# One statically planned instruction stream for two mixed attention branches, in place of two phases with a filler list

## The chip, the cores and the metric

The kernel runs on one core of a Trainium2 chip. The metric is the device time of one execution in microseconds (us), from the first instruction to the last. A core has five engines that run side by side, each through its own instruction stream in order: TensorE (PE in the profile, its weight loads PEld), ScalarE (ACT), VectorE (DVE), GpSimd (POOL) and the queue that issues transfers (SP).[...]

## The reference

The input is one sequence of 2048 tokens with 640 features; there are 32 heads of 20. Branch A is a linear attention whose feature map is a softmax over each head's 20 features, of `+p` and of `-p`. Branch B is causal attention within four segments of 512 tokens, mixed with a memory that is updated from segment to segment. A gate per token mixes the two.

```python
# A: q,k,v = x @ wqkv ; pq = q @ w_phi ; pk = k @ w_phi      (per head)
phi_q = concat([softmax(pq), softmax(-pq)], -1)
phi_k = concat([softmax(pk), softmax(-pk)], -1)
kv  = einsum('bhsf,bhsd->bhfd', phi_k, v);  z = phi_k.sum(s)
o   = (phi_q @ kv) / (phi_q @ z + 1e-6);    a = o.reshape(B,S,D) @ wo
# B: for each of 4 segments of L=512
logits = q k^T * Dh**-0.5 + mask            # mask: -1e9 above the diagonal
a_dot  = softmax(logits) @ v
a_mem  = phi(q) @ M / (phi(q) @ z + 1e-6)   # phi(t) = t+1 if t>0 else exp(t)
o = g_h * a_mem + (1 - g_h) * a_dot
M += phi(k)^T v ;  z += phi(k).sum           # then b = o @ wo
out = gate * a + (1 - gate) * b              # gate = sigmoid((x * gate_w).sum(-1))
```

## The kernel before

It works in two phases. Phase one loads and transposes x, folds `w_phi` into the k and q weights of A, and runs A over the 16 chunks of 128 tokens (`a1_v`, `a1_k`, `a1_kv`). Phase two is a loop over 32 steps, one for each segment and each group of four heads of B; the order of TensorE's stream is written by hand, and units of other work (the projections of the next segment, A's second half, the output projection) are put between its parts from a list sorted by a position. The order on the other engines is left to the framework.

```python
def mm_x(ps, sc, W, lo, hi):                      # one projection of 128 tokens, 5 matmuls
    for c in range(KC):
        nc.tensor.matmul(ps, lhsT=xT[:, c, sc * P:(sc + 1) * P], rhs=W[:, c, lo:hi],
                         start=(c == 0), stop=(c == KC - 1))
...
def b_k(s, c):                                    # K of B: project, store, load transposed
    for hf in range(2):
        ps = wtile("kb_ps")
        mm_x(ps[:, 0:320], sc, WkB, 320 * hf, 320 * hf + 320)
        nc.vector.tensor_copy(out=kp[:, hf * 16:hf * 16 + 16, 0:DH], in_=...)
    nc.sync.dma_start(out=kd[s][rows, :], in_=kp.rearrange("p h d -> p (h d)"))
    nc.sync.dma_start_transpose(out=kT2[s % 2][:, :, rows], in_=kd[s][rows, :])
...
def b_q(s, g):                                    # Q of B comes out transposed from TensorE
    ps = wtile("qb_ps")
    for c in range(KC):
        nc.tensor.matmul(ps, lhsT=WqB[:, c, 4 * g:4 * g + 4, :],    # heads padded 20 -> 32
                         rhs=xT[:, c, s * L:(s + 1) * L], ...)
    nc.vector.tensor_copy(out=qT, in_=ps)
...
POFF = {0: 0, 1: 512, 3: 896, 2: 1024}
def b_qk(qT, kT, PT, cs):                         # called with (0,), (1, 3), (2,)
    st2 = [pst.tile([P, 2, 512], F32, name="st") for _ in range(2)]   # pst: 2 x 2 banks
    for c in cs:
        for i in range(4):                        # four heads, 32 rows of the array each
            nc.tensor.matmul(st2[i // 2][:, i % 2, o:o + n], lhsT=kT[r:r + 32, ...],
                             rhs=qT[r:r + 32, c * P:L], ..., tile_position=(r, 0))
    for pr in range(2):
        nc.scalar.activation(out=PT[:, 2 * pr:2 * pr + 2, base:base + w],
                             in_=st2[pr][:, :, 0:w], func=ACT.Exp, scale=SCALE_B)
    for c in cs:                                  # causal mask of the diagonal block
        view = PT[:, :, POFF[c]:POFF[c] + P]
        nc.gpsimd.affine_select(out=view, in_=view, pattern=[[0, 4], [1, P]],
                                compare_op=ALU.is_ge, fill=0.0, base=0,
                                channel_multiplier=-1)
def b_pv(...):   # 40 matmuls of 21 columns: lhsT a 128x128 block of PT, rhs = [v, 1]
def b_mem(...):  # 4 matmuls read the memory M, 4 update it, and two small VectorE operations
...
def a3_pq(s, g):   # 6 groups of 6 heads: 5 matmuls of 512 columns, then exp(+), exp(-)
def a3_num(...):   # numerator and denominator of A in one set of matmuls, 22 columns a head
def fin_mm(...):   # 10 matmuls of 320 columns, a ScalarE copy, the store of the output
...
for k in range(NG):                               # 32 steps
    for t, cs in enumerate(((0,), (1, 3), (2,))):
        b_qk(qT, kT, PT, cs)
        if t == 0 and k + 1 < NG:
            nxt = b_q(*divmod(k + 1, G))
        ...                                       # b_mem / b_pv / b_epi of step k-1
        while fill and fill[0][0] < k + SHARE[t]:
            fill.pop(0)[1]()
```

Of the kernel before, what the change touches and what calls it, by code (L numbers as in the profile page):

```python
# [11 lines left out]
AX = mybir.AxisListType  # L12

@with_exitstack
def kernel(
# [16 lines left out]
    P = 128  # L32
    S = 2048
    D = 640
    H = 32
    DH = 20
    KC = D // P
    NCH = S // P
    NSEG = 4
    L = S // NSEG  # L40
    G = H // 4
    SCALE_B = DH ** (-0.5)
    NG6 = 6
    GW = [120] * 5 + [40]
    GH = [6] * 5 + [2]
    EKW = 1376
    V1 = DH + 1

    x2 = A_x[0]
    out2 = out[0]  # L50
    PSUM = bass.MemoryType.PSUM

    class Seg:
        pass

    const = ctx.enter_context(tc.tile_pool(name="const", bufs=1))
    bres = ctx.enter_context(tc.tile_pool(name="bres", bufs=1))
    bkw = ctx.enter_context(tc.tile_pool(name="bkw", bufs=2))
    dram = ctx.enter_context(tc.tile_pool(name="dram", bufs=1, space=bass.MemoryType.DRAM))
    kd = [dram.tile([L, H * 32], BF16, name=f"kd{s}") for s in range(NSEG)]  # L60
    od = [[dram.tile([L, D], BF16, name=f"od{s}_{X}") for X in range(2)] for s in range(NSEG)]
    psw = ctx.enter_context(tc.tile_pool(name="psw", bufs=4, space=PSUM))
    psa_stack = ExitStack()
    psa = psa_stack.enter_context(tc.tile_pool(name="psa", bufs=1, space=PSUM))
    apool_stack = ExitStack()
    apool = apool_stack.enter_context(tc.tile_pool(name="apool", bufs=1, side="right"))
    a1w = apool_stack.enter_context(tc.tile_pool(name="a1w", bufs=3, side="right"))
    ctx.enter_context(tc.manual_schedule(engines={mybir.EngineType.PE}))

    def wtile(name, dt=F32):  # L70
        if dt == BF16:
            return psw.tile([P, 1024], BF16, name=name, tag="w")
        return psw.tile([P, 512], F32, name=name, tag="w")

    xT = const.tile([P, KC, S], BF16, name="xT")
    xv = x2.rearrange("(c p) d -> p c d", p=P)
    x_nat = apool.tile([P, 4, D], BF16, name="x_nat")
    wnat_k = apool.tile([P, KC, D], BF16, name="wnat_k")
    wnat_q = apool.tile([P, KC, D], BF16, name="wnat_q")
    Wc = apool.tile([P, NG6, DH], BF16, name="Wc")  # L80
    WvA = apool.tile([P, KC, D + 1], BF16, name="WvA")
    gw_row = apool.tile([KC, P], BF16, name="gw_row")
    beta_b = const.tile([P, H], BF16, name="beta_b")
    WkB = bres.tile([P, KC, D], BF16, name="WkB")
    WvB = bres.tile([P, KC, D], BF16, name="WvB")
    WqB = bres.tile([P, KC, H, 32], BF16, name="WqB")
    WoA = bres.tile([P, KC, D], BF16, name="WoA")
    WoB = bres.tile([P, KC, D], BF16, name="WoB")
    wphi_rows = A_w_phi.rearrange("h f g -> (h f) g")
    nc.vector.memset(Wc[:, NG6 - 1, :], 0.0)  # L90

    def wload(dst, src):
        nc.sync.dma_start(out=dst, in_=src.rearrange("(c p) n -> p c n", p=P))

    nc.sync.dma_start(out=x_nat[:, 0:2], in_=xv[:, 0:2, :])
    nc.sync.dma_start(out=gw_row, in_=gate_w.rearrange("(c p) -> c p", p=P))
    nc.sync.dma_start(out=Wc[0:120, 0:5, :],
                      in_=wphi_rows[0:600, :].rearrange("(c p) g -> p c g", p=120))
    nc.sync.dma_start(out=Wc[0:40, 5, :], in_=wphi_rows[600:640, :])
    nc.sync.dma_start(out=x_nat[:, 2:4], in_=xv[:, 2:4, :])  # L100
    wload(WvA[:, :, 0:D], A_wqkv[:, 2 * D:3 * D])
    wload(wnat_k, A_wqkv[:, D:2 * D])
    for sc in range(4, NCH):
        nc.sync.dma_start_transpose(out=xT[:, :, sc * P:(sc + 1) * P],  # L104
                                    in_=x2[sc * P:(sc + 1) * P, :])
    wload(wnat_q, A_wqkv[:, 0:D])
    wload(WkB, B_wk)
    wload(WvB, B_wv)
    wq_st = []
    for c in range(KC):  # L110
        w = a1w.tile([P, D], BF16, name="wq_st", bufs=2)
        nc.sync.dma_start(out=w, in_=B_wq[c * P:(c + 1) * P, :])
        wq_st.append(w)
    wload(WoA, A_wo)
    wload(WoB, B_wo)
    nc.sync.dma_start(out=beta_b, in_=B_beta.partition_broadcast(P))

    ident_f = const.tile([P, P], F32, name="ident_f")
    nc.gpsimd.memset(ident_f, 0.0)
    nc.gpsimd.affine_select(out=ident_f, in_=ident_f, pattern=[[-1, P]],  # L120
                            compare_op=ALU.not_equal, fill=1.0, base=0,
                            channel_multiplier=1)
    ident_b = const.tile([P, P], BF16, name="ident_b")
    nc.vector.tensor_copy(out=ident_b, in_=ident_f)

    def block_mask(name, n, step, width, parts):
        m = const.tile([P, n], F32, name=name)
        nc.gpsimd.memset(m, 1.0)
        nc.gpsimd.affine_select(out=m, in_=m, pattern=[[-step, n]], compare_op=ALU.is_ge,
                                fill=0.0, base=0, channel_multiplier=1)  # L130
        nc.gpsimd.affine_select(out=m, in_=m, pattern=[[step, n]], compare_op=ALU.is_ge,
                                fill=0.0, base=width - 1, channel_multiplier=-1)
        return m

    m6 = block_mask("m6", 6, DH, DH, 120)
    bd4 = block_mask("bd4", 4, 32, 32, P)
    ind = const.tile([P, 4], BF16, name="ind")
    nc.vector.tensor_copy(out=ind, in_=bd4)

    EkNs = []  # L140
    for i in range(4):
        e = apool.tile([P, EKW], BF16, name=f"EkN{i}")
        nc.gpsimd.memset(e[:, 1280:EKW], 0.0)
        EkNs.append(e)
    WkA = apool.tile([P, KC, D], BF16, name="WkA")
    WqA = const.tile([P, KC, 728], BF16, name="WqA")
    nc.gpsimd.memset(WqA[:, :, D:728], 0.0)
    nc.gpsimd.memset(WqB[:, :, :, DH:32], 0.0)

    kpads = []  # L150
    for b in range(3):
        kp = bres.tile([P, H, 32], BF16, name=f"kpad{b}")
        nc.gpsimd.memset(kp[:, :, DH:32], 0.0)
        kpads.append(kp)
    kT2 = [bres.tile([P, G, L], BF16, name=f"kT{b}") for b in range(2)]
    phik2, vB2 = [], []
    for b in range(2):
        pk = bres.tile([P, 4, H, 32], BF16, name=f"phik{b}")
        vb = bres.tile([P, 4, H, V1], BF16, name=f"vB{b}")
        nc.gpsimd.memset(pk[:, :, :, DH:32], 0.0)  # L160
        nc.gpsimd.memset(vb[:, :, :, DH:V1], 1.0)
        phik2.append(pk)
        vB2.append(vb)
    Msb = bres.tile([P, G, 4, V1], F32, name="Msb")
    nc.gpsimd.memset(Msb, 0.0)
    nc.gpsimd.affine_select(out=Msb[:, :, :, DH], in_=Msb[:, :, :, DH],
                            pattern=[[0, G], [-32, 4]], compare_op=ALU.not_equal,
                            fill=1e-6, base=-DH, channel_multiplier=1)
    Mbd = bres.tile([P, G, 4, V1], BF16, name="Mbd")

    Wphi = apool.tile([P, NG6, 6, DH], BF16, name="Wphi")
    nc.vector.tensor_tensor(out=Wphi[0:120],
                            in0=Wc[0:120, :, None, :].to_broadcast([120, NG6, 6, DH]),
                            in1=m6[0:120, None, :, None].to_broadcast([120, NG6, 6, DH]),
                            op=ALU.mult)

    class Fold:
        pass

    def fold_new(wn, dst, nm):  # L180
        f = Fold()
        f.wn, f.dst = wn, dst
        f.WT = apool.tile([P, NG6, KC, P], BF16, name=f"WT{nm}", tag="WT")
        return f

    def fold_tr(f, g):
        gw = GW[g]
        tp = wtile("wtp", BF16)
        for ic in range(KC):
            nc.tensor.transpose(out=tp[0:gw, ic * P:(ic + 1) * P],  # L190
                                in_=f.wn[:, ic, g * 120:g * 120 + gw], identity=ident_b)
        src = tp[0:gw, 0:D].rearrange("p (c k) -> p c k", k=P)
        if g % 2 == 0:
            nc.scalar.copy(out=f.WT[0:gw, g], in_=src)
        else:
            nc.vector.tensor_copy(out=f.WT[0:gw, g], in_=src)

    def fold_mm(f, ic):
        for (g0, g1) in ((0, 4), (4, 6)):
            ps = wtile("wfold")  # L200
            for g in range(g0, g1):
                gw = GW[g]
                o = (g - g0) * 120
                nc.tensor.matmul(ps[:, o:o + gw], lhsT=f.WT[0:gw, g, ic, :],
# [519 lines left out]
```

The softmax here doesn't subtract the row's maximum and nothing guards it: scores larger than these inputs give would overflow.

## Time and profile before

| | |
|---|---|
| device time | 417.99 us, median of 3 runs (416.78 to 420.93) |
| span of the profiled execution | 415.1 us, 9891 instructions, mean granted TensorE clock 0.951 |
| instructions | 3930 matmuls, 503 on ScalarE, 608 on VectorE, 366 on GpSimd |
| transfers | 30.04 MB in 59137 packets; the one transfer queue fills 27.4% of the 16 engines' time |
| from memory / to memory | 7.24 MB read, 11.40 MB written |

How to read it: the profile gives each engine's busy time as a share of the span, the busy share in 40 equal slices (a digit is tenths), the chain of work that ended last, and groups of instructions with the time their engine stood idle just before them and what released it. A busy TensorE isn't a TensorE at its peak, since matmuls overlap and their ends are modelled.

### The profile page before, as it was taken

The page shows a single profiled execution, that of the slowest core. Times are in us where ns is not written, and L with a number is a line of the kernel's source. Part 1 is how long each engine was busy: PE and PEld are TensorE (multiplying, and loading weights), DVE is VectorE, ACT ScalarE, POOL GpSimd, SP SyncE. Part 2 cuts the span into 40 slices and gives each one's busy share as a digit, 9 for nine tenths or more (in the row PEclk, how much of TensorE's full clock was granted, in tenths as well). Part 3 has the DMA queues.
Part 4 walks back from the last instruction along what each step waited for, and adds up shares of the span by engine and source line. Part 5 has one row for each costly group of instructions (what it writes and reads, how often), then busy time and mean ns, then how long its engine had stood idle before and what let it go on. Part 6 is the DMA issues. An engine that isn't in the chain of part 4 may idle for free.

```text
span 415.1 us, 9891 instructions
## 1 busy us (share of the span) xinstructions
PE 340.2 (82%) x3930; PEld 215.7 (52%) x3961; DVE 234.2 (56%) x608; ACT 271.7 (65%) x503; POOL 209.1 (50%) x366
## 2 busy tenths in 40 slices
PE   2996999967788858789889888789988798876686
PEld 1674777755344534445455545356554355444454
DVE  4336856769246635557587456376664555466620
ACT  1573666721777757888677886568877597976402
POOL 9026797891225444545545454353554464657510
PEclk9998999999999989899999999899998899999659
DMA  8887000005301204217211213821020162100311
GB/s 235 145 251 260 2 3 2 2 25 153 77 26 27 54 14 86 49 59 151 72 51 48 53 49 105 148 73 53 30 56 2 34 159 65 49 13 5 112 42 55
DMA packets 59137, 30.04 MB, mean 72 GB/s; under 512 B 45779, under 2 KB 57043, under 8 KB 59091
## 3 DMA queue, kind: packets, MB, share of 16 engines
q1 hardware_dynamic: 59091, 29.41, 27.4%
q8 instruction: 31, 0.51, 0.5%
q14 instruction: 15, 0.12, 0.1%
HBM read 7.24 MB, written 11.40 MB: 45 GB/s over the span
## 4 chain that ended last, share of the span: by engine, by line
PE 42%; ACT 19%; DVE 13%; POOL 10%; SPq 6%; issue 5%; DMA 4%; POOLq 0%; DVEq 0%; ACTq 0%
ACT PT L431 14%; PE o_ps L578 10%; PE qb_ps L399 6%; SPq L104 4%; POOL PT L435 4%; PE st L425 4%; PE vb_ps L237 4%; PE pq_ps L503 4%; DMA wq_st<-in_B_wq_dram 3%; PE kb_ps L237 3%; PE nd_ps L445 3%; PE va_ps L237 2%; PE ka_ps L237 2%; POOL EkN L265 2%; DVE ts L541 2%
## 5 line engine op out<-in xcount | busy, mean ns | idle before, releaser
L431 ACT ACTIVATE PT<-st 128x1024 bf16<-128x1024 f32 (+1 forms) x192 | 158.4, 884 | 22.8 <-PE st L425 19.1
L435 POOL TENSOR_SCALAR_AFFINE_SELECT PT<-PT 128x512 bf16<-128x512 bf16 x128 | 80.6, 642 | 108.4 <-ACT PT L431 95.4
L237 PEld LDWEIGHTS <-xT 128*128 128x128 bf16 x640 | 61.2, 100 | 32.4 <-issue 3.3
L425 PE MATMUL st<-qT,kT 32*128 32x128 bf16 (+3 forms) x512 | 48.2, 313 | 21.0 <-ACT PT L431 18.9
L265 POOL TENSOR_TENSOR EkN<-Ek,krec 128x1280 bf16<-128x1280 bf16 x16 | 37.7, 2359 | 25.6 <-DVE krec L264 23.8
L445 PE MATMUL nd_ps<-vB,PT 128*128 128x21 bf16 x1280 | 42.8, 173 | 3.0 <-POOL PT L435 1.4
L403 DVE CAST qT<-qb_ps 128x512 bf16<-128x512 f32 x32 | 22.1, 691 | 40.7 <-PE qb_ps L399 40.7
L578 PEld LDWEIGHTS <-oT 128*128 128x128 bf16 x320 | 32.2, 104 | 22.8 <-issue 4.1
L445 PEld LDWEIGHTS <-PT 128*128 128x128 bf16 x1280 | 36.7, 96 | 14.0 <-issue 6.1
L399 PE MATMUL qb_ps<-xT,WqB 128*128 128x512 bf16 x146 | 40.1, 396 | 4.5 <-DVE ts L541 2.6
L425 PEld LDWEIGHTS <-kT 32*128 32x128 bf16 x512 | 15.6, 92 | 50.3 <-issue 47.6
L546 POOL TENSOR_TENSOR oA<-ts 128x360 bf16<-128x360 f32 (+1 forms) x32 | 27.5, 861 | 25.9 <-DVE ts L541 24.8
L582 ACT CAST osb<-o_ps 128x320 bf16<-128x320 f32 x32 | 13.6, 425 | 38.3 <-PE o_ps L578 37.9
L578 PE MATMUL o_ps<-WoA,oT 128*128 128x320 bf16 x160 | 29.7, 320 | 4.6 <-ACT Eq L507 1.6
L503 PE MATMUL pq_ps<-xT,WqA 128*128 128x512 bf16 x103 | 29.6, 388 | 3.9 <-DVE tm L482 1.6
L578 PE MATMUL o_ps<-WoB,oT 128*128 128x320 bf16 x160 | 30.2, 324 | 2.9 <-DMA oT<-od 2.9
L237 PE MATMUL vb_ps<-WvB,xT 128*128 128x320 bf16 x160 | 25.8, 310 | 5.4 <-DVE Msb L469 2.1
L541 DVE TENSOR_TENSOR ts<-num_ps,cs 128x360 f32<-128x360 f32 (+1 forms) x64 | 28.4, 483 | 2.1
L478 DVE RECIPROCAL rd<-nd_ps 128x16 f32<-128x16 f32 x32 | 8.0, 249 | 34.6 <-PE nd_ps L445 34.5
L247 ACT CAST vA<-va_ps 128x320 bf16<-128x320 f32 x32 | 13.6, 425 | 20.5 <-PE va_ps L237 20.5
L257 ACT ACTIVATE Ek<-ka_ps 128x320 bf16<-128x320 f32 x64 | 23.1, 440 | 5.9 <-PE ka_ps L237 5.5
L237 PE MATMUL va_ps<-WvA,xT 128*128 128x320 bf16 (+1 forms) x160 | 26.8, 318 | 0.1
(109 smaller groups left out, 573.8 us busy)
## 6 DMA issues: line engine op xcount, KB each, us to landing
kd<-kpad SPq DMA_DIRECT2D x16, 256.0 KB, 2.4
od<-oA SPq DMA_DIRECT2D x16, 160.0 KB, 1.8
out_dram<-osb SPq DMA_DIRECT2D x16, 160.0 KB, 1.8
od<-oB SPq DMA_DIRECT2D x12, 160.0 KB, 2.2
WvA<-in_A_wqkv_dram SPq DMA_DIRECT2D x1, 800.0 KB, 5.6
wnat_k<-in_A_wqkv_dram SPq DMA_DIRECT2D x1, 800.0 KB, 7.4
wnat_q<-in_A_wqkv_dram SPq DMA_DIRECT2D x1, 800.0 KB
WkB<-in_B_wk_dram SPq DMA_DIRECT2D x1, 800.0 KB, 6.7
```

Source lines behind the costliest of these rows:

```text
L237: nc.tensor.matmul(ps, lhsT=xT[:, c, sc * P:(sc + 1) * P], rhs=W[:, c, lo:hi], start=(c == 0), stop=(c == KC - 1))
L257: nc.scalar.activation(out=Ek[:, sgn, 320 * hf:320 * hf + 320], in_=ps[:, 0:320], func=ACT.Exp, scale=1.0 if sgn == 0 else -1.0)
L265: nc.gpsimd.tensor_tensor(out=EkNs[sc % 4][:, 0:1280].rearrange("p (h f) -> p h f", f=DH), in0=Ek.rearrange("p s (h f) -> p (s h) f", f=DH ...
L399: nc.tensor.matmul(ps, lhsT=WqB[:, c, 4 * g:4 * g + 4, :], rhs=xT[:, c, s * L:(s + 1) * L], start=(c == 0), stop=(c == KC - 1))
L425: nc.tensor.matmul(st2[i // 2][:, i % 2, o:o + n], lhsT=kT[r:r + 32, c * P:(c + 1) * P], rhs=qT[r:r + 32, c * P:L], start=True, stop=True, ...
L431: nc.scalar.activation(out=PT[:, 2 * pr:2 * pr + 2, base:base + w], in_=st2[pr][:, :, 0:w], func=ACT.Exp, scale=SCALE_B)
L435: nc.gpsimd.affine_select(out=view, in_=view, pattern=[[0, 4], [1, P]], compare_op=ALU.is_ge, fill=0.0, base=0, channel_multiplier=-1)
L445: nc.tensor.matmul(nd[:, j * 84 + i * V1:j * 84 + (i + 1) * V1], lhsT=PT[:, i, o:o + P], rhs=vb[:, c, 4 * g + i, :], start=(j == 0 and i = ...
L503: nc.tensor.matmul(ps, lhsT=WqA[:, c, g * 120:g * 120 + P], rhs=xT[:, c, s * L:(s + 1) * L], start=(c == 0), stop=(c == KC - 1))
L541: nc.vector.tensor_tensor(out=ts[:, sgn, 0:nh, :], in0=pss[sgn][:, :, 0:DH], in1=cs[:, sgn, 0:nh, None].to_broadcast([P, nh, DH]), op=ALU. ...
L546: nc.gpsimd.tensor_tensor(out=segs[s].oA[qc][:, h0 * DH:(h0 + nh) * DH].rearrange("p (h d) -> p h d", d=DH), in0=ts[:, 0, 0:nh, :], in1=ts ...
L578: nc.tensor.matmul(ps[:, 0:320], lhsT=segs[s].oT[qc, X][:, k5, :], rhs=Wo[:, k5, hf * 320:hf * 320 + 320], start=(n == 0), stop=(n == 2 * ...
```

## The change

The change rewrites the kernel. Every piece of work becomes an operation with an engine (or a choice of ScalarE and VectorE), an assumed duration, a priority key and the tiles that it reads and writes. When the program is built, a list scheduler plays these durations forward and writes down one order for all engines; nothing of it runs on the chip. The purpose is to overlap branch B's attention, which needs ScalarE, with branch A's first half, which the kernel before had as a phase of its own.

```diff
+class Planner:
+    HOP = {"PE": 0.27, "ACT": 0.20, "DVE": 0.18, "POOL": 0.13, ...}   # assumed handover
...
+def pe_t(n):  return max(n / 2400 + 0.0025, 0.025)
+def act_t(n, psum=True): return (0.05 if psum else 0.093) + 0.000833 * n
...
-    psw = ctx.enter_context(tc.tile_pool(name="psw", bufs=4, space=PSUM))
-    pst = ctx.enter_context(tc.tile_pool(name="pst", bufs=2, space=PSUM, ...))   # later
-    ctx.enter_context(tc.manual_schedule(engines={mybir.EngineType.PE}))
+    st4 = ps.tile([P, 4, 512], F32, name="st4")
+    wt = [ps.tile([P, 512], F32, name=f"w{i}") for i in range(4)]
+    ctx.enter_context(tc.manual_schedule())
...
+    def b_kq(s, c, key):                     # K and Q of B, both by rows of tokens
+        for X, Wn in enumerate(("WkB", "WqB")):
+            for hf in range(2):
+                bk = proj(4 * s + c, Wn, (Wn,), hf, key)        # 5 matmuls of 320
+                op(AD, cp_t(320), copy_to(... T["kq"][i][..., X, :, 0:DH] ...))
+        dma(... kd[s][rows, :] <- T["kq"][i] ..., kb=524)
+    def kq_get(s, g, key):                   # 32 of these; [512, 256] -> [128, 2, 512]
+        dma(lambda: nc.sync.dma_start_transpose(out=T["kqT"][j],
+                                        in_=kd[s][:, g * 256:(g + 1) * 256]), ...)
...
+    def grp(s, g, i):                        # five score tiles for two groups of heads
+        return (((g, 0, 0),), ((g, 1, 0), (g, 3, 384)), ((g, 2, 0), (g + 1, 2, 256)),
+                ((g + 1, 0, 0),), ((g + 1, 1, 0), (g + 1, 3, 384)))[i]
+    def b_qk(n, s, prods, slot):             # 80 of these
+        ... nc.tensor.matmul(st4[:, i, o:o + w], ..., tile_position=(r, 0))
+        op("ACT", act_t(2048), lambda: nc.scalar.activation(
+            out=T["PT"][slot], in_=st4, func=ACT.Exp, scale=SCALE_B), ...)
+        for _, _, o in prods:
+                v = T["PT"][slot][:, :, o:o + P]
+                nc.gpsimd.affine_select(out=v[:, :, 0:8], in_=v[:, :, 0:8],
+                                        pattern=[[0, 4], [1, 8]],
+                                        compare_op=ALU.is_ge, fill=0.0, base=0,
+                                        channel_multiplier=-1)
...
+    def b_upd_(s, q, key):                   # memory update for 16 heads at once
+    def a3_pq(s, t, key):                    # 5 blocks of 128 features, not 6 of 120
+    def a3_den(s, qc, key):                  # denominators apart: 10 matmuls of 14-16 columns
+    def a3_num(s, qc, hf, key):              # numerators: 3 matmuls per sign and half
+    def kv_pass(p, key):                     # state of A once for 4 chunks, not per chunk
...
-    for k in range(NG): ...                  # the loop of 32 steps and its filler list
+    seg_in(0, ...); fold("k", ...); a1_four(0); att_seg(0); seg_in(1, ...); a1_four(1); ...
+    pl.run(wt)
```

Three things besides the order are changed. Q of branch B is no longer made transposed by TensorE with padded weights: it is projected like K, stored beside it in memory and loaded back transposed. The exponential of the scores takes all four banks (2048 columns) in one instruction, with one such tile instead of two half-sized ones. And the causal select covers the first 8 of the 128 columns of each diagonal block instead of all 128: the changed kernel leaves out the mask on the other 120 columns, so there later keys of the same block count in the softmax. Copies out of PSUM go to ScalarE or VectorE, as the planner chooses; the transposed loads of x and of the q weights, and the weights, are issued from SP and ACT.

## The prediction

> **What bounds the kernel now.** I read the page's first part and its slices first, to see which engine is near full and when.
>
> ```profile
> PE 340.2 (82%) x3930; PEld 215.7 (52%) x3961; DVE 234.2 (56%) x608; ACT 271.7 (65%) x503; POOL 209.1 (50%) x366
> PE   2996999967788858789889888789988798876686
> ACT  1573666721777757888677886568877597976402
> PEclk9998999999999989899999999899998899999659
> ```
>
> TensorE is the fullest engine, yet 75 us of the 415.1 us span are idle on it (415.1 - 340.2). The second row tells where: full from slice 3 to 8, about eight tenths afterwards, ragged at both ends. So I asked for the busy time by stretch; the columns are busy us (instructions) of PE, PEld, DVE, ACT and POOL, then the clock, the transfer share and GB/s.
>
> ```profile
> 40.00:82.00 42.00, 41.64 (x519) 32.48 (x518) 30.50 (x47) 28.92 (x81) 33.30 (x51) 0.99 0.02 6
> 82.00:150.00 68.00, 51.07 (x543) 30.93 (x544) 38.95 (x93) 37.38 (x65) 30.04 (x58) 0.97 0.21 55
> 150.00:350.00 200.00, 170.32 (x2059) 100.66 (x2083) 117.79 (x351) 151.97 (x249) 99.64 (x172) 0.96 0.29 70
> 350.00:392.00 42.00, 32.82 (x423) 20.00 (x425) 25.12 (x73) 31.41 (x60) 24.30 (x47) 0.92 0.14 40
> 392.00:400.00 8.00, 5.01 (x73) 3.63 (x70) 3.65 (x11) 0.38 (x1) 3.95 (x6) 0.53 0.28 66
> 400.00:415.10 15.10, 11.82 (x83) 8.05 (x81) 0.98 (x2) 3.40 (x8) 0.00 (x0) 0.91 0.13 45
> ```
>
> Branch A's first half (40 to 82) is TensorE-bound at 99%. The seam between the phases (82 to 150) loses 16.9 us, the long attention stretch 29.7 us, 350 to 392 loses 9.2 us, the last 23 us lose 6.3 us; the first 40 us, not shown, lose 12.4 us (8.2 up to 14 us, 4.3 after). None of the attention stretches has an engine above 85%: they are held by handovers. The chain of what ended last and the waits name them (us in total, times, longest):
>
> ```profile
> PE 42%; ACT 19%; DVE 13%; POOL 10%; SPq 6%; issue 5%; DMA 4%; POOLq 0%; DVEq 0%; ACTq 0%
> ```
>
> ```profile
> POOL PT L435 <- ACT PT L431: 95.4, 54, 10.8
> ...
> ACT PT L431 <- PE st L425: 19.1, 20, 5.4
> PE st L425 <- ACT PT L431: 18.9, 36, 1.9
> ```
>
> Scores, exponential and mask hand over in a ring, though GpSimd's 95.4 us of waiting is only idleness of an engine that isn't the bound. The bound is TensorE's work plus some 75 us of starting, seam and handover.
>
> **What the Trainium skill says.** "Perfetto Trace Analysis", section Optimization Strategy: where the most contended engine changes over time, performance "may be improved by interleaving those regimes". The stretches agree that the regime changes: 99% of TensorE and 69% of ScalarE (28.92 of 42) in branch A, 85% and 76% in attention. The change does just this. The same page, section Optimizing Scalar/DVE Operations, puts the fixed cost of a ScalarE operation at about 51 ns on PSUM, and says that the profiled latency is longer because its second half overlaps the next instruction. The timeline agrees: two exponentials of 1024 columns show as 1.84 us together, 0.92 each, while a single one measures 1.021. "TensorE: Matmul & The Clock Gate", section Back-to-back issue gap, gives N/2.4 + 2.5 ns; at 320 columns that is 136 ns, and the chain has ten such matmuls in 1.36 to 1.37 us. So the planner's assumed durations, which have the same form, are near this chip's. The same page, What's actually happening, says the clock halves after an idle window; the row from 392 to 400 agrees, 5.01 us busy of 8 and a clock of 0.53.
>
> **The change, part by part.** These are the rows that price it (busy us, mean ns | idle before it).
>
> ```profile
> L431 ACT ACTIVATE PT<-st 128x1024 bf16<-128x1024 f32 x128 | 123.9, 1021 | 21.5 <-PE st L425 17.9 <-issue 2.1 <-POOL oB L492 0.7
> L399 PE MATMUL qb_ps<-xT,WqB 128*128 128x512 bf16 x146 | 40.1, 396 | 4.5 <-DVE ts L541 2.6 <-issue 1.6
> L431 ACT ACTIVATE PT<-st 128x512 bf16<-128x512 f32 x64 | 35.4, 610 | 1.3 <-PE st L425 1.2
> L503 PE MATMUL pq_ps<-xT,WqA 128*128 128x512 bf16 x103 | 29.6, 388 | 3.9 <-DVE tm L482 1.6
> L237 PE MATMUL kb_ps<-WkB,xT 128*128 128x320 bf16 x160 | 24.2, 299 | 0.0
> L281 PE MATMUL zt<-ind,EkN 128*128 128x4 bf16 x192 | 15.5, 165 | 0.0
> L277 PE MATMUL acc<-vA,EkN 128*128 128x120 bf16 x160 | 14.8, 214 | 7.0 <-POOL EkN L265 7.0
> ```
>
> *TensorE.* Q of B stops computing the padding of 20 to 32: it becomes as large as K, 24.2 in place of 40.1, so -15.9. A's q features come in 5 blocks instead of 6: 29.6 x 20/24 = 24.7, so -4.9. A's state: acc and zt cost 34.0 now (14.8 and 15.5, and 3.7 for the narrow blocks); 160 matmuls at 92 ns and 160 at 81 ns (busy over count) are 27.7, so -6.3. The separate denominators add 160 small matmuls at zt's 81 ns, +12.9. Scores, p times v, the output projection and the other projections keep their matmuls. Sum -14.2: 340 becomes 326.
>
> *ScalarE and VectorE.* The slope between the two forms of the exponential is (1021 - 610)/512 = 0.80 ns a column; the pair's 0.92 plus 1024 columns at 0.83 ns, taken on the slow side, makes about 1.8 to 1.9 for 2048. 80 x 1.87 = 150 in place of 159. The other exponentials that must be on ScalarE come to 73 at today's durations (23.1 Ek, 23.8 for 40 of 24 x 2 Eq, 15.1 eq, 8.9 ek, 2 small), 223 in all; what must be on VectorE I add up to 185. Some 205 copies at 0.43 to 0.49 us (90 us) go to either. (223 + 185 + 90)/2 = 249 on each, if well shared: 69% of the predicted time. Neither becomes the bound.
>
> *GpSimd.* The selects shrink from 512 to 32 columns (8 for each of four heads). The smallest one with 32 columns in the trace took this long:
>
> ```profile
> 10.04 0.26 POOL L166 TENSOR_SCALAR_AFFINE_SELECT Msb<-Msb 128x32 f32<-128x32 f32 x1
> ```
>
> 128 x 0.26 = 33 in place of 80.6, and about 0.4 us less between an exponential and the p times v that needs it. That is work left out: the mask of 120 columns in each diagonal block. GpSimd goes from 209 to about 160.
>
> *Transfers.* Stores of K become K with Q, 512 KB for 256 KB, sixteen times; transposed loads of them go from 16 to 32 of 256 KB. That is 8 MB more on 30, so the transfer share goes from 27% towards 40%, and SP issues 16 more transposes at 1.24 us. Hidden, except at the start of a segment, where store (2.4 us landing), issue and load (3.3) stand in a row before the first scores.
>
> *Idle on TensorE.* Start: 12 of today's 12.4 stay, for the same bytes must land. The seam goes, since attention of segment 0 begins at about 28 us by my count (weights, projections of segment 0, round trip) and A's chunks run beside it: 3 of 16.9. In the middle I take 5% of some 300 us, 15, in place of 38.9 (29.7 + 9.2), for the planner always has matmuls without a near dependency to put into a gap. End: 6 as now. Together 36 in place of 75, -39.
>
> 326 + 36 = 362. The part that I choose rather than read is the 5%.
>
> **The rivals.** *The ring of one score tile.* Before, there are two score tiles and ScalarE waits 19 us for them in total; now one tile of four banks holds TensorE out while the exponential reads, and ScalarE out while TensorE fills. The shortest turn is 1.87, about 0.25 to hand back, 0.3 to 0.4 for the matmuls, 0.1 to hand on: 2.6 us, 80 turns are 210. With a start at 28 and an end of 20 that is 258, not a bound. But both queues are in order; if other work in front of the turn costs 1.7 us on each, the ring takes 345 and the time is about 395. For it: the 18.9 us that TensorE waits for exponentials already. Against: other ScalarE work, 99 us, needs such gaps anyway.
>
> *A fixed order that fits an assumed chip.* If durations or handovers differ (a copy measures 425 to 489 ns alone, against 317 to 398 assumed), every engine meets its queue's head too early, and only four work banks cover it. With today's 15% of idle in the attention stretches kept throughout, 326/0.85 + 18 = 402. Against: back-to-back spacing, not latency, is what the planner assumes, and that agreed above.
>
> *Transfers in one queue.* If a segment's round trip (some 7 us) stands bare four times, and loads of x and weights delay the start by 10, 362 becomes 400. For it: the transfer share is 0.8 in the first fifth already. Against: A's work is there to be run meanwhile.
>
> A better outcome: TensorE 95% full after 30 us, and the clock nearer 1 because it never idles, 345.
>
> **Range and chances.** 362 us, 8 in 10 between 340 and 398. The three rivals end at 395 to 402, still more than 2% under 418; slower needs two of them at once. Faster by over 2%: 0.87; within 2%: 0.06; slower: 0.07.
>
> **What would show it.** TensorE busy about 326 at 88 to 92% of the span; 80 exponentials of 2048 at about 1.87; selects near 0.26; ScalarE and VectorE 65 to 72% each; no stretch like the seam. If ScalarE's waits for scores plus TensorE's for exponentials exceed 60 us, the ring is the bound; if TensorE's waits are spread over many VectorE and ScalarE copies, the fixed order is; if they name kqT, the transfers are. I am wrong if TensorE's busy time doesn't fall, or its idle stays near 75.

## The result and the profile after

The changed kernel takes 335.38 us (median of 12 runs, 334.29 to 338.11) against 417.63 us before (15 runs beside it). The ratio is 0.804, with a 95% interval of 0.8015 to 0.8067. The prediction of 362 us had the direction, but the time lies below its range: the gain is 82 us and not 56.

First the page of the changed kernel, the same rows as shown of before: busy times, then two slice rows.

```profile
PE 302.5 (91%) x3991; PEld 209.5 (63%) x4002; DVE 224.2 (67%) x568; ACT 252.7 (76%) x330; POOL 151.1 (45%) x338
PE   2799998999999988998999898998998998979996
...
PEclk9999997999999999999999999999999999965999
```

TensorE is busy for 302.5 us in 332.6, 91%, and idle for 30.1 in place of 74.9. The ragged parts of its row, the seam and the end, are mostly gone. The same in stretches (busy us and instructions of PE, PEld, DVE, ACT, POOL, then clock, transfer share, GB/s):

```profile
0.00:40.00 40.00, 30.96 (x243) 21.52 (x244) 14.97 (x41) 22.22 (x46) 10.18 (x36) 1.00 0.74 212
40.00:82.00 42.00, 39.97 (x541) 27.97 (x539) 32.06 (x61) 35.60 (x44) 24.03 (x44) 0.96 0.56 106
82.00:150.00 68.00, 65.07 (x894) 47.44 (x894) 56.97 (x123) 54.36 (x84) 37.26 (x70) 1.00 0.27 71
150.00:300.00 150.00, 137.60 (x2035) 92.25 (x2047) 112.65 (x327) 126.95 (x138) 72.41 (x175) 0.98 0.56 121
300.00:332.60 32.60, 28.91 (x290) 20.28 (x289) 7.60 (x21) 13.54 (x20) 7.25 (x15) 0.89 0.27 76
```

ScalarE is now at 80 to 85% in the three middle stretches, where before it had 69% in branch A's part: the two regimes run together. The waits round the scores (total us, times, longest) answer to those shown of before:

```profile
POOL PT L892 <- ACT PT L886: 58.9, 34, 4.5
ACT PT L886 <- PE st L880: 18.3, 22, 2.9
PE st L880 <- ACT PT L886: 3.1, 8, 1.0
```

ScalarE waits for scores as long as before (18.3 against 19.1), though there is one tile. What fell is the third row, TensorE waiting for an exponential before it can write scores: 18.9 to 3.1 us. And the rows of the operations that the prediction priced:

```profile
L886 ACT ACTIVATE PT<-st 128x2048 bf16<-128x2048 f32 x80 | 151.2, 1890 | 19.4 <-PE st L880 18.3 <-POOL PT L892 0.6
...
L892 POOL TENSOR_SCALAR_AFFINE_SELECT PT<-PT 128x32 bf16<-128x32 bf16 x128 | 30.8, 252 | 61.2 <-ACT PT L886 58.9 <-DMA out_dram<-osb 2.2
...
L502 PE MATMUL w<-WqB,xT 128*128 128x320 bf16 x160 | 25.4, 299 | 1.0 <-DVE WqA L457 0.6 <-DVE ts L791 0.4
```

1.890 us against 1.87 for the exponential, 0.252 against 0.26 for the select, 25.4 against 24.2 for Q: the single prices held.

### The profile page after: what moved, and what is told of

It reads as the page before. It is cut to its first block, busy times and chain, and to the rows that moved or that the text cites. A ratio compares the mean times of both kernels' runs of the same rounds, so it can differ in the third digit from the quotient of the medians.

```text
span 332.6 us, 9836 instructions
## 1 busy us (share of the span) xinstructions
PE 302.5 (91%) x3991; PEld 209.5 (63%) x4002; DVE 224.2 (67%) x568; ACT 252.7 (76%) x330; POOL 151.1 (45%) x338
## 4 chain that ended last, share of the span: by engine, by line
PE 51%; DVE 22%; ACT 13%; issue 5%; POOL 5%; DMA 3%; SPq 1%; ACTq 0%; DVEq 0%; POOLq 0%
PE w L502 22%; PE w L832 11%; ACT PT L886 8%; PE w L906 5%; PE st L880 4%; DVE ts L791 3%; PE w L724 3%; DMA beta_b<-in_B_beta_dram 3%; POOL EkN L613 2%; ACT Ek L599 2%; ACT Eq L732 2%; DVE ksum L607 2%; DVE rm L925 1%; DVE phik L531 1%; DVE phiq L863 1%
## 5 line engine op out<-in xcount | busy, mean ns | idle before, releaser
L886 ACT ACTIVATE PT<-st 128x2048 bf16<-128x2048 f32 x80 | 151.2, 1890 | 19.4 <-PE st L880 18.3
L892 POOL TENSOR_SCALAR_AFFINE_SELECT PT<-PT 128x32 bf16<-128x32 bf16 x128 | 30.8, 252 | 61.2 <-ACT PT L886 58.9
L613 POOL TENSOR_TENSOR EkN<-Ek,krec 128x1280 bf16<-128x1280 bf16 x16 | 37.7, 2356 | 12.0 <-DVE krec L611 8.9
L906 PE MATMUL w<-vB,PT 128*128 128x21 bf16 x1280 | 37.3, 173 | 2.2 <-DVE ts L791 0.8
L962 POOL TENSOR_TENSOR oB<-td,tm 128x320 bf16<-128x320 f32 x24 | 21.4, 894 | 37.3 <-DVE td L930 37.3
L880 PE MATMUL st<-kqT 32*128 32x384 bf16 (+3 forms) x512 | 32.8, 310 | 3.3 <-ACT PT L886 3.1
L795 POOL TENSOR_TENSOR oA<-ts 128x320 bf16<-128x320 f32 x32 | 27.7, 870 | 15.9 <-DVE ts L791 15.2
L791 DVE TENSOR_TENSOR ts<-w,cs 128x320 f32<-128x320 f32 x64 | 28.4, 481 | 2.4 <-POOL oA L795 1.4
L502 PE MATMUL w<-WkB,xT 128*128 128x320 bf16 x160 | 27.6, 320 | 2.2 <-ACT xT L438 2.1
L832 PE MATMUL w<-WoA,oTA 128*128 128x320 bf16 x160 | 28.4, 309 | 0.1
L832 PE MATMUL w<-WoB,oTB 128*128 128x320 bf16 x160 | 27.8, 305 | 0.0
L502 PE MATMUL w<-WvA,xT 128*128 128x320 bf16 x160 | 25.4, 299 | 1.6 <-DVE vB L457 0.7
L502 PE MATMUL w<-WqB,xT 128*128 128x320 bf16 x160 | 25.4, 299 | 1.0 <-DVE WqA L457 0.6
```

What stands on the lines that cost most here:

```text
L502: nc.tensor.matmul(w[:, 0:width], lhsT=T["xT"][:, c, sc * P:(sc + 1) * P], rhs=T[Wn][:, c, 320 * hf:320 * hf + width], start=(c == 0), sto ...
L613: op("POOL", pool_t(1280), lambda: nc.gpsimd.tensor_tensor(out=T["EkN"][ie].rearrange("p (h f) -> p h f", f=DH), in0=v3(), in1=T["krec"][j ...
L791: op("DVE", dve_t(320), lambda w, sgn=sgn: nc.vector.tensor_tensor(out=T["ts"][d][:, sgn], in0=w[:, 0:320].rearrange("p (h d) -> p h d", d ...
L832: nc.tensor.matmul(w[:, 0:320], lhsT=T[nm][j][:, k5, :], rhs=T[Wo][:, k5, hf * 320:hf * 320 + 320], start=(i == 0), stop=(i == 9))
L880: nc.tensor.matmul(st4[:, i, o:o + w], lhsT=T["kqT"][j][r:r + 32, 0, c * P:(c + 1) * P], rhs=T["kqT"][j][r:r + 32, 1, c * P:L], start=True ...
L886: op("ACT", act_t(2048), lambda: nc.scalar.activation(out=T["PT"][slot], in_=st4, func=ACT.Exp, scale=SCALE_B), r=("st4",), w=(("PT", slot ...
```

## The experiments

My theory after the result: TensorE remains the bound, and most of the gain is that it no longer stands still or waits inside its stream. The rivals: fewer and cheaper instructions make the gain (columns, mask, tile), or the ring of scores and exponentials sets the time. Medians are of 4 runs unless said; differences are from 335.4 us for edits of the changed kernel and from the runs of before beside it for edits of the kernel before. An execution more than 1.5% above the fastest of its kernel counts as slow, and the ratios leave such ones out, so that a ratio and two medians can differ a little. The changed kernel itself did not run again beside its edits; before did, on four chips, with medians of 417.7 to 419.1 us, so differences of 1 or 2 us are not resolved.

**The whole mask again.**

```diff
-nc.gpsimd.affine_select(out=v[:, :, 0:8], in_=v[:, :, 0:8], pattern=[[0, 4], [1, 8]],
+nc.gpsimd.affine_select(out=v, in_=v, pattern=[[0, 4], [1, P]],
```

> The changed kernel with the select over all 128 columns of each diagonal block again, in the same order of all engines. If the gain comes from TensorE's fuller stream (my theory), GpSimd goes from 151 to about 200 us busy (128 x 0.39 us more) and the time rises by under 4 us, to 335 to 340. If the smaller mask is a main cause (rival: selects on the way from exponential to p times v), it rises by 12 us or more.

339.8 us (337.2 to 343.4), +4.4, with GpSimd busy for 203.1. That is hardly over what my theory allowed and far from the 12 of the rival. This version masks as the reference does; it is 0.811 of before (0.804 to 0.818), so the work left out explains about a twentieth of the gain or less.

**Two score tiles, two exponentials.**

```diff
-    st4 = ps.tile([P, 4, 512], F32, name="st4")
+    sth = [ps.tile([P, 2, 512], F32, name=f"st{i}") for i in range(2)]
-        op("ACT", act_t(2048), ... out=T["PT"][slot], in_=st4 ...)
+        for h in range(2):
+            op("ACT", act_t(1024), ... out=T["PT"][slot][:, 2*h:2*h+2], in_=sth[h] ...)
```

> The changed kernel with two score tiles of two banks and two exponentials of 1024 columns in place of one of four banks and 2048, planned anew. If filling four heads at once from one released tile is what cut the score matmuls' busy time from 48 to 33 us (theory), it returns to 43 to 50 us and the time rises by 6 to 15 us. If the busy time fell only because the stream is better filled (rival), the score matmuls stay under 37 us and the time stays within 4 us; ScalarE's extra fixed cost is 80 x 0.05 = 4 us, off the path.

349.2 us (346.6 to 352.2), +13.8, but the score matmuls are busy for 37.3 us and don't return to 43 or more (32.8 in the changed kernel, 48.2 before). The time moved as my theory said and its sign in the profile didn't; the run had also been planned anew, so the next two runs change the plan alone.

**Only the plan changes.** One assumed duration, nothing else.

```diff
-        op("ACT", act_t(2048), lambda: ...
+        op("ACT", 2 * act_t(1024), lambda: ...       # 1.756 -> 1.806
```

> A control for the run with two score tiles: the changed kernel with the same instructions, planned anew because one assumed duration, that of the exponential of four banks, goes from 1.756 to 1.806 us (twice that of 1024 columns). If the two-tile run's 13.8 us are the cost of two tiles (theory), this run stays within 4 us of the changed kernel, 332 to 339. If they are the loss of a plan that its priorities were not tuned for (rival), this run is slower by 8 us or more too.

342.9 us (340.8 to 343.8), +7.5. Neither expectation fits fully: the plan alone makes half of what I had put down to two tiles. The other direction:

```diff
+        op("ACT", act_t(2048) - 0.05, lambda: ...    # 1.756 -> 1.706
```

> A second control of the plan: the same instructions as the changed kernel, with the assumed duration of the four-bank exponential 0.05 us shorter (1.706) in place of 0.05 longer. If the 7.5 us that the first control lost are the distance from a plan that its priorities were tuned for (theory), this one is slower than 335.4 too, by 3 to 10 us. If the assumed duration was simply too short, and longer is better or worse in one direction (rival), this run is at or under 335.

338.4 us (336.6 to 339.0), +3.0; by the ratio to before, 0.807 (0.803 to 0.811), this one can't be told from the changed kernel's 0.804. So a plan made anew costs 0 to 7.5 us here, and 11.0 in another run below, and every edit that makes the planner run anew may carry that much. Of the 13.8 us of two tiles, 6 to 11 remain by these two runs and 3 by the worst plan: that one tile gains in the new order is likely, its size isn't shown.

**Q's columns.** Matmuls of 512 columns of which 320 are used, the plan held.

```diff
-                                 rhs=T[Wn][:, c, 320 * hf:320 * hf + width],
+                n = real or width                     # real=512 for WqB
+                                 rhs=T[Wn][:, c, 320 * hf - lo:320 * hf - lo + n],
```

> The changed kernel with Q of B projected with 512 columns a matmul, as wide as before, of which 320 are used; the order is the same. 160 matmuls x 192 columns at 2.4 a ns are 12.8 us more for TensorE. If TensorE is the bound (theory), the time rises by 10 to 14 us. If the ring of scores and exponentials or the handovers set the time (rival), the columns fill gaps and it rises by under 5 us.

343.5 us (343.3 to 345.2), +8.2 for 12.8 us of columns. Between the two expectations and nearer to TensorE as the bound: 64% of added work becomes time. TensorE's busy row:

```profile
PE 316.0 (92%) x4002; PEld 208.9 (61%) x4002; DVE 222.4 (65%) x568; ACT 253.2 (74%) x330; POOL 151.2 (44%) x338
```

It rose by 13.5, so the columns cost what they should, and idle gave 2.6 back (30.1 to 27.5).

**Half of the exponentials.** The other two heads' p are constants; this leaves work out.

```diff
-            out=T["PT"][slot], in_=st4, func=ACT.Exp, ...
+            out=T["PT"][slot][:, 0:2], in_=st4[:, 0:2], func=ACT.Exp, ...
```

> The changed kernel in the same plan, but each exponential of scores reads only two of the four banks (1024 of 2048 columns); the other two heads' p are constants. It leaves out half of the exponentials: 80 x 0.85 = 68 us of ScalarE's work, and it shortens each turn of the ring by 0.85 us. If the ring of one score tile or ScalarE sets the time (rival), it falls by 25 us or more. If TensorE sets it (theory), it falls by under 10 us, with TensorE's busy share at 93% or more.

```profile
PE 306.2 (91%) x4002; PEld 209.5 (63%) x4002; DVE 227.4 (68%) x568; ACT 188.8 (56%) x330; POOL 156.1 (47%) x344
```

ScalarE's busy time falls from 252.7 to 188.8, and the time is 336.8 us (336.5 to 337.0), not lower at all. Neither the ring nor ScalarE sets the time in this order. I had looked for a busy share of 93% on TensorE; it stays at 91%, so what keeps it idle isn't the exponential.

**The regimes one after the other.** The first scores of B wait for A's last state; A's chunks, and the loads of x for them, come early.

```diff
-    a1_four(0)
-    att_seg(0)
+    for p in range(4):
+        a1_four(p)
+    a1_state(A1K[15] + 4)
+    att_seg(0)                # in b_qk: r = ... + (("KVa", i) for i in 0..3) if n == 0
```

> The changed kernel, planned so that the first scores of B wait for the last state of A: the two regimes follow one another as in the kernel before, with all else of the change kept. If the interleaving is the main gain (theory), the time rises by 25 to 50 us, to 360 to 385, with TensorE full in A's part and under 88% in attention. If fewer and cheaper instructions are the main gain (rival), it rises by under 12 us.

365.0 us (363.1 to 366.7), +29.6: as the theory of interleaving had it. Two stretches of it show the old picture, A's half and then the first attention:

```profile
80.00:110.00 30.00, 29.10 (x357) 22.38 (x356) 19.75 (x43) 19.96 (x43) 20.47 (x41) 1.00 0.14 54
110.00:150.00 40.00, 30.98 (x480) 21.07 (x477) 19.01 (x53) 33.48 (x30) 5.97 (x26) 0.80 0.32 81
```

With nothing of A left to run beside it, attention leaves TensorE 77% busy, and the granted clock falls to 0.80. Over the whole run (365.0 us of span) TensorE's idle time rises by 17.6 us, 30.1 to 47.7, and its busy time by 14.8, 302.5 to 317.3, for the same instructions at a mean clock of 0.911 in place of 0.974: about half of the loss is waiting and half a slower clock. This order too was planned anew, so some us of the 29.6 may be the plan and not the sequence.

**The kernel before with one score tile.**

```diff
-        st2 = [pst.tile([P, 2, 512], F32, name="st") for _ in range(2)]
+        st = pst.tile([P, 4, 512], F32, name="st")       # bufs=1, one exponential
```

> The kernel before with the changed kernel's score tile: one tile of four banks and one exponential for it, at most 2048 columns, in the old hand-written order. If one tile is good by itself because four heads are filled at once (theory of cheaper scores), the score matmuls' busy time falls from 48 to under 38 us and the time by 4 to 12 us. If it pays only where other work fills the turn (theory of order), TensorE's wait for exponentials goes from 19 to over 60 us and the time rises by 15 us or more.

421.4 us (20 runs) beside 417.9, ratio 1.002 (0.998 to 1.006; 6 of the 20): no gain. Neither expectation holds: each has its change in the profile, though the wait less than half as large as expected, and the two cancel.

```profile
PE st L425 <- ACT PT L430: 30.8, 38, 2.7
ACT PT L430 <- PE st L425: 29.4, 35, 5.5
```

The score matmuls' busy time falls from 48.2 to 36.0, while the waits of TensorE for exponentials rise from 18.9 to 30.8, as much. In the old order the tile gives nothing. That it needs an order which brings the scores only when the tile is free is my reading; TensorE's wait for exponentials, 3.1 us in the planned order, fits it.

**The kernel before with the small mask.**

```diff
-            view = PT[:, :, POFF[c]:POFF[c] + P]           # pattern [[0, 4], [1, P]]
+            view = PT[:, :, POFF[c]:POFF[c] + 8]           # pattern [[0, 4], [1, 8]]
```

> The kernel before with the select over the first 8 columns of each diagonal block, as in the changed kernel: the mask of the other 120 columns is left out. GpSimd falls by some 50 us. If the select lies on the way to p times v (the chain of before puts 4% of the span, 17 us, on it), the time falls by 6 to 15 us; if GpSimd is hidden, by under 3 us.

411.5 us beside 417.9, ratio 0.983 (0.978 to 0.988): 6 us, at the lower end of the expected 6 to 15. So in the old order the select is on the path for some of its time; that it costs more there than in the new order (6 against some 4) is within the noise.

**The kernel before with less of Q.** Three of five matmuls; two fifths of the sum are left out.

```diff
-        for c in range(KC):
+        for c in range(3):
```

> The kernel before with three of the five matmuls in each projection of Q of B; it leaves out two fifths of that sum. 64 matmuls of 512 columns, at 0.2165 us, are 13.9 us less for TensorE, about what the change saves there. If TensorE's work sets the time in the old order too, it falls by 8 to 14 us. If its waits swallow it (rival), by under 5 us.

411.0 us beside 418.1, ratio 0.983 (0.978 to 0.988): 7.1 for 13.9 us of columns, 51%, between both expectations.

**Four parts undone at once**: the regimes in sequence, two tiles, the whole mask, the wide Q; each edit as above.

> The changed kernel with four parts taken back at once: B's first scores wait for A's last state, two score tiles of two banks, the full causal select, and Q of B projected with 512 columns a matmul. If the effects add (29.6 + 13.8 + 4.4 + 8.2 = 56), the time is 391, 385 to 397, and 26 us of the gain belong to the rest of the rewrite. If they overlap (rival: once TensorE waits, columns, mask and tile are hidden in its waits), it stays under 378.

383.5 us (383.0 to 384.4), +48.1, between the two expectations. It is 8 less than the sum of the single effects, but that doesn't show an overlap: the sum counts the cost of a new plan twice (in the 13.8 and the 29.6), and this run bears it once. Of the gain of 82, some 34 belong to something else.

**The planned order for TensorE alone.**

```diff
-    ctx.enter_context(tc.manual_schedule())
+    ctx.enter_context(tc.manual_schedule(engines={mybir.EngineType.PE}))
```

> The changed kernel with the planned order for TensorE alone, the same row for row; ScalarE, VectorE, GpSimd and SP go in the order that the framework chooses, as in the kernel before. If the planned order of all engines is the rest of the gain (theory), TensorE's gaps grow and the time rises by 15 us or more, to 350 to 380. If TensorE's own order carries it (rival), it stays within the spread of the plans, 333 to 346.

369.7 us (367.0 to 373.3), +34.3, ratio to before 0.882 (0.875 to 0.888), with TensorE's stream the same row for row: against the framework's order, the planned order of the other engines is worth about as much as the interleaving. TensorE's longest waits, in the longest of the four runs:

```profile
PE w L444 <- ACT xT L438: 11.5, 1, 11.5
PE st L880 <- ACT PT L886: 10.5, 13, 1.4
PE w L429 <- DMA x_nat<-in_A_x_dram: 6.5, 2, 4.5
```

Part of the loss is one event at the start: the framework lets SP issue all transposed loads of x ahead, ScalarE's copy of the first x chunk waits 18.5 us for such a load, and TensorE is 22.0 us busy in the first 40 instead of 31.0. The rest of the idle time, 19.5 us of 28.5, is spread over short waits, of which the scores' wait for exponentials, 3.1 us in the full plan, is the largest.

**Plans for other chips.** The same instructions with modelled durations of ScalarE and VectorE at 0.8; with handovers doubled; with durations that the trace shows.

```diff
+    return 0.8 * ((0.05 if psum else 0.093) + 0.000833 * n)              # fastchip; dve_t too
+    HOP = {"PE": 0.54, "ACT": 0.40, "DVE": 0.36, "POOL": 0.26, ...}       # hop2
+        op("DVE", 0.58, ...phik...); op("DVE", 0.74, ...); op("ACT", 1.82, ...) ...   # measured
```

> The same instructions, planned for a chip on which every ScalarE copy and exponential and every VectorE operation with a modelled duration takes 0.8 of what was assumed. If assumed durations near the chip's are what keeps TensorE from waiting (theory of a fitted order), the gaps of TensorE grow by 10 us or more and the time to 347 or beyond. If any order of this kind does (rival: what counts is the amount of independent work, not the fit), it stays inside the spread of the two controls, under 344.

> The same instructions, planned with every assumed handover between engines twice as long (TensorE's 0.54 in place of 0.27 us, and so on): consumers stand later in each queue. Fitted order: 340 to 352, with fewer waits inside the stream but more work at the end. Rival of amount: within the controls, 333 to 344.

> The same instructions, planned with the durations that the trace shows where the assumed ones were off most: the feature maps of B on VectorE (0.58 and 0.74 in place of 0.24 and 0.40; 0.27 and 0.48 in place of 0.20 and 0.34), the masked memory (0.7 in place of 0.41) and the exponential (1.82 in place of 1.76). If the fit of durations governs (theory of a fitted order), it gains, to 328 to 334. If the tuned priorities govern (rival), it falls within the controls, 336 to 344.

346.4 us (344.1 to 348.5), 343.3 (343.1 to 344.5) and 338.2 (336.8 to 340.1). The plan for a faster chip loses 11.0, between its two expectations (TensorE idles 7.5 us more, not 10), and 3.5 more than the worse of the two runs that change the plan alone. Doubled handovers land where both expectations allow. Measured durations do not gain, against the theory of a fitted order. So a planned order is robust to errors of this size: none of the five other plans is further than 11 us away, and none is better than the one whose priorities were tuned. No version here beats the changed kernel.

## Why the prediction was wrong, step by step

**The step that failed is the sum for TensorE**, "Sum -14.2: 340 becomes 326". Measured: 302.5, -37.7. That term makes 23.5 us of the 29.4 between the predicted 362 and the 332.6 of the profiled span; the idle time makes the other 5.9. The mechanism, that interleaving takes away TensorE's waiting, was right. Two errors lie in the sum, and a part of it stays open.

*It held the clock constant.* The product of busy time and granted clock behaves like TensorE's work: 340.2 x 0.951 = 323.5 before, 302.5 x 0.974 = 294.6 after. In the runs with one quantity changed it follows the columns: 316.0 x 0.975 = 308.1 for the wide Q, 13.5 more for 12.8 us of columns; 332.6 x 0.933 = 310.3 for the short Q, 13.2 less for 13.9. In the nine other runs with the changed kernel's matmuls and one score tile or two it lies between 293.0 and 296.9, though their busy times differ by 14 us (299.9 to 313.8); only the serial run, at 289.1, falls outside. By it the work fell by 28.9, which at before's clock is 30.4 us, and the other 7.3 us of busy time are the higher clock. The prediction named a clock nearer 1 only for its better outcome; it belonged in the sum.

*It took busy time for work.* "Scores ... keep their matmuls" was right in number but not in time. These are the rows of before, of before with one tile, and of the changed kernel:

```profile
L425 PE MATMUL st<-qT,kT 32*128 32x128 bf16 (+3 forms) x512 | 48.2, 313 | 21.0 <-ACT PT L431 18.9 <-DVE qT L403 0.8
L425 PE MATMUL st<-qT,kT 32*128 32x128 bf16 (+3 forms) x512 | 36.0, 312 | 31.7 <-ACT PT L430 30.8 <-DVE qT L403 0.9
L880 PE MATMUL st<-kqT 32*128 32x384 bf16 (+3 forms) x512 | 32.8, 310 | 3.3 <-ACT PT L886 3.1
```

One matmul lasts as long in all three (313, 312, 310 ns). What changes is how many run side by side. Each uses 32 rows of the array, and four heads that start together take no longer than two; here are four of 512 columns, before in two rows and after in one (start, duration):

```profile
204.70 0.39 PE L425 MATMUL st<-qT,kT 32*128 32x512 bf16 x2 [0.30 <-ACT PT L431]
205.19 0.39 PE L425 MATMUL st<-qT,kT 32*128 32x512 bf16 x2
201.50 0.40 PE L880 MATMUL st<-kqT 32*128 32x512 bf16 x4
```

Before, the two half-sized tiles came free one after the other, and so did their heads. In the changed kernel all four start together. One tile alone does this in the old order (36.0), and with the regimes in sequence it is 35.9 with one tile and 47.5 with two (the run with four parts undone). In the interleaved order two tiles cost less, 37.3; there TensorE waits only 1.9 us for exponentials before scores. By the product one tile is worth 8 us in the old order (340.4 x 0.927 = 315.6) and 2 in the new (two tiles: 296.9).

Busy time over count also priced small matmuls wrongly, for records overlap. Before, the 4-column matmuls stood between wider ones:

```profile
62.07 0.23 PE L277 MATMUL acc<-vA,EkN 128*128 128x120 bf16 x1
62.13 0.17 PE L281 MATMUL zt<-ind,EkN 128*128 128x4 bf16 x1
62.16 0.21 PE L277 MATMUL acc<-vA,EkN 128*128 128x120 bf16 x1
62.22 0.17 PE L281 MATMUL zt<-ind,EkN 128*128 128x4 bf16 x1
```

From one pair to the next is 0.08 to 0.09 us here, not 92 + 81 = 173 ns, the price I gave it: by spacing the pairs cost half. In the changed kernel 40 of the small ones are one row:

```profile
149.80 1.14 PE L650 MATMUL w<-ind,EkN 128*128 128x4 bf16 x40
```

1.08 us to the next row, 27 ns each; the planner's own `pe_t`, with its 25 ns at the least, was nearer than my 81. So A's state hardly changed (-6.3 was an artefact), and the denominators, at that spacing, cost some 4 us and not 12.9. The two errors cancel in part: +6.6 together in the sum, some +4 by spacing.

*What is left.* Of the 28.9, Q is about 13 (the two runs on columns) and one tile 2 to 8. A's five blocks in place of six save 20 of 120 matmuls, 4 us at spacing, and the denominators give that back. So 8 to 14 us I can't place. The row of p times v fell by 5.5 us, from 42.8 to 37.3, with the same 1280 matmuls, which the prediction also took as unchanged. TensorE's gaps fell from 86 to 41 in number, and the last record before a gap stands alone, 0.17 us for a 21-column matmul that follows its neighbour by 0.025; as an estimate, 45 gaps fewer are some 7 us. But the serial run has 51 gaps and the smallest product of all, so the cause of this part stays open.

**Idle, predicted -39, measured -44.8.** In microseconds its parts held: the seam's stretch 2.9 us (predicted 3), the middle 14.4 (15), the start 9.0 (12), the end 3.7 (6). The middle owes this in part to luck: I took 5% of some 300 us, and from 40 to 300 us, the seam's stretch included, TensorE idles for 17.3 of 260, 6.7%. The serial run shows where the gain comes from: without A to fill in, idle is 47.7 us in place of 30.1.

**ScalarE and VectorE** were predicted at 249 each: 252.7 and 224.2. Neither is the bound, as the half exponentials show for ScalarE. GpSimd, predicted about 160, has 151. Transfers: 45.0% and 3.5% of the engines' time on two queues, against "towards 40%"; apart from 6.5 us of waiting for x at the start, none of TensorE's longer waits names a transfer.

**The rivals.** The ring isn't the bound (half exponentials: no gain). The fixed order on an assumed chip: real, but 0 to 11 us and not 40. Transfers: none of those waits names kqT. The rivals put the range's upper end at 398 and the middle too high; the upside had one case, 345, which had the clock but not the scores that start in fours. Where the prediction reads the row from 392 to 400 as a clock that halves after an idle window, it reads too much: TensorE's longest gap from 376 to 400 us is 2.1 us.

**What the prediction also had wrong without it showing:** it turned TensorE's work into time one for one. Measured, it is 51% in the old order and 64% in the new, so the columns brought some 7 to 8 us. The greater part came from order: 30 us for interleaving, 34 for the planned order of the other engines, by taking each back, less what a new plan costs by itself in the first. These two were not taken back together, so how far they overlap is open.

## What to carry to other kernels

Where one engine is 80% busy and no other is full, price the order before the instructions: here taking back the planned order of the other engines cost 34 us and taking back the interleaving 30, while 13 us of removed matmul columns were worth 7 to 8. Multiply TensorE's busy time by the granted clock before comparing two profiles, and price small matmuls by the distance from start to start, for busy time over count counts overlap twice. A single change can be without effect in one order and have one in another, as the one score tile probably did, and when a planner runs anew, a run with only the plan changed tells what the replanning itself costs.

## What the runs showed of the hardware

The granted clock on one core moved between 0.902 and 0.990 among runs of nearly the same instructions. In the clock records of the traces it is at every moment full or half, in stretches that are multiples of 3.41 us: before, 41 us of the span were at half clock, in the changed kernel 17, in the serial run 65. Laid over TensorE's busy time, all 17 traces together show 105 changes from full to half, and none after a window of 3.41 us in which TensorE was busy for over 85% (median 62%); where the clock stayed full the median was 100%. So TensorE's clock went with many short gaps, none of 3.41 us needed: the serial run's stretch at 0.80 has 9 us idle of 40. That the idle time causes the change was not tried by itself, and windows of 46 to 85% also kept the full clock.

Four score matmuls in four sets of 32 rows took 0.40 us for 512 columns each, and two took 0.39. VectorE's minimum in the feature map of K took 822 ns for 640 columns in the changed kernel against 607 before, with one operand now also the output; the cause was not looked for.
